# Decode attention with a gated feed-forward: how w_down, wo and the last V tiles are cut into DMAs

## The chip, the core and the metric

The kernel runs on one core of one Trainium2 chip. The metric is the time of one execution on the device in microseconds (us). The kernel before was timed in three runs: 2534.33 us median, from 2534.22 to 2534.78.

## The reference

One token attends over a cache of 65,536 positions with 32 heads of 128; a small feed-forward block works on the same token, and a scalar gate mixes the two. All inputs are bf16.

```python
# x: (1, 1, 512); k_cache, v_cache: (1, 32, 65536, 128); wq: (512, 4096); wo: (4096, 512)
q = (x @ wq).reshape(B, Sq, H, Dh).transpose(0, 2, 1, 3)
scores = jnp.einsum("bhqd,bhkd->bhqk", q, k_cache) * (Dh ** -0.5)
p = softmax(scores, axis=-1)
o = jnp.einsum("bhqk,bhkd->bhqd", p, v_cache)
a = o.transpose(0, 2, 1, 3).reshape(B, Sq, H * Dh) @ wo

# w_gate, w_up: (512, 1792); w_down: (1792, 512)
b = (silu(x @ w_gate) * (x @ w_up)) @ w_down

g = sigmoid((x * gate_w).sum(-1, keepdims=True))
out = g * a + (1 - g) * b
```

The two caches are 512 MiB each; everything else together is about 13 MiB.

## The kernel before, in words

**Tiles.** K and V of a head are each cut into four tiles of 16,384 positions, so there are N = 128 tiles of K and 128 of V. A tile is 128 partitions of 32 KB (NB = 128 positions of 128 values each), 4 MB in all. The tiles live in a ring of five slots of that size (`take` hands out the slot that came free first, `give` returns one). Weights that are needed for a while borrow a ring slot: wq in the beginning (`wq_t`), then w_gate and w_up together (`gu_t`), w_down (`wd_t`), and at the end the second half of wo (`wo_late`).

**Work on a tile.** For a K tile, VectorE multiplies it in place by q (L254) and halves the products by additions (L258); TensorE then adds the rest of each product in PSUM with the identity as weights (`scores`, L267), and VectorE folds four columns to one (L281). When a head's four tiles are scored, its softmax follows (L287 to L300). For a V tile, TensorE multiplies four columns of weights at a time (`values`, L322, 32 matmuls a tile). When a head's four V tiles are done, its 4x512 sums are copied (L335), turned into a column (`head_turn`, L351), scaled (L358) and multiplied by the head's rows of wo (`project`, L365) into two PSUM rows that gather all heads.

**The order.** The code is written in the order in which every engine works (`manual_schedule`). First four K tiles are scored, with the queries, the gate and the feed-forward block in between; then a loop over `steps` loads K tile n, the rows of wo that are due, and V tile v, and works on both. V runs some tiles behind K, so the last steps hold V alone.

**SP's queue.** Every large transfer is issued by SyncE (SP), in program order; SP waits at a DMA until its slot is free. The DMAs take eight completion semaphores in turn, the two small ones of ScalarE's queue at the start first, so an issue also waits until the DMA eight places ahead of it has landed. Up to the loop, SP's queue holds in this order: wq's first columns (L100), K tiles 0 to 2 (L110), the rest of wq (L382), w_gate (L387), K tile 3 (L110), w_up (L389), six DMAs of w_down (L402), K tile 4, two more DMAs of w_down, V tile 0; then K tile 5 and V tile 1, K tile 6 (into w_down's slot, so behind the matmuls of L233), the first wo rows (L163), V tile 2, and so on.

**w_down before.** Its 1792 rows lie on 64 partitions of 28 rows (28,672 contiguous bytes each). Eight DMAs carry it, each with eight partitions, one out of every four (first, first + 4, ... first + 28, for first = 0, 1, 2, 3, 32, 33, 34, 35). Since the hidden vector comes out on 128 partitions of 14 values (`hT`), two matmuls with every other column of the identity (L227) and a copy (L231) bring it to 64 partitions of 28, and 28 matmuls (L233) follow.

**wo before.** Heads 0 to 15 come four at a time (`WG = 4`), 512 KB in rows of 1 KB, one step or so ahead of use. Heads 16 to 31 (`LATE = 16`) come as 2 MB in four DMAs (L169) behind the last V tile, in cuts of 5, 5, 4 and 2 heads; their projections all run at the very end (L480).

**The last V tiles before.** V tiles 125 and 126 come in two halves, V tile 127 in pieces of 32, 32, 32, 16, 8 and 8 positions (`V_CUTS`). The last eight positions are not multiplied with the rest but turned at once into the head's column (L343).

The lines that the prediction's steps touch: `load` (L104 to L111), `load_wo` and `load_late` (L160 to L170), `feed_forward_out` (L223), `project` (L362), the start of the queue (L380 to L416), the loop (L432 to L481) and the output (L484 to L486).

Of the kernel before, what the change touches and what calls it, by code (L numbers as in the profile page):

```python
# [8 lines left out]
ACT = mybir.ActivationFunctionType  # L9
ALU = mybir.AluOpType  # L10
AXIS = mybir.AxisListType
P = 128
# [3 lines left out]
NB = 128  # L16
# [6 lines left out]
LAG = 8  # L23
SPREAD = 40

WG = 4
LATE = 16
LATE_CUTS = (0, 5, 10, 14, LATE)
TURNED = 8
V_CUTS = {3: (0, 64, NB), 2: (0, 64, NB), 1: (0, 32, 64, 96, 112, NB - TURNED, NB)}  # L30


@with_exitstack
def kernel(
# [14 lines left out]
    nc = tc.nc  # L49
    bf16 = mybir.dt.bfloat16  # L50
    f32 = mybir.dt.float32

    _, H, Sk, Dh = A_k_cache.shape
    D = A_x.shape[2]
    F = B_w_gate.shape[1]
    KT = D // P
    FT = F // P
    G = Sk // (NB * P)
    NBH = Sk // P
    N = H * G  # L60
# [4 lines left out]
    consts = ctx.enter_context(tc.tile_pool(name="consts", bufs=1))  # L65
# [7 lines left out]
    psum_m = ctx.enter_context(tc.tile_pool(name="psum_m", bufs=2, space=bass.MemoryType.PSUM))  # L73
# [7 lines left out]
    def take(name):  # L81
        slot = free.pop(0)
        held[name] = slot
        return ring.tile(
            [P, NB * Dh], bf16, name=name.split(".")[0], tag=f"slot{slot}"
        )

    def give(name):
        free.append(held.pop(name))
# [14 lines left out]
    def load(dst, cache, n, name, cuts=(0, NB), slot=None):  # L104
        h, g = divmod(n, G)
        t = take(f"{name}.{n}") if slot is None else slot
        view = t.rearrange("p (j d) -> p j d", d=Dh)
        src = cache[0, h, g * NB * P : (g + 1) * NB * P, :].rearrange("(p j) d -> p j d", j=NB)
        for a, b in zip(cuts[:-1], cuts[1:]):
            nc.sync.dma_start(out=view[:, a:b, :], in_=src[:, a:b, :])  # L110
        dst[n] = view  # L111

    def load_k(n):
        load(K_tiles, A_k_cache, n, "K_t")

    def load_v(n):
        load(V_tiles, A_v_cache, n, "V_t", V_CUTS.get(N - n, (0, NB)))

# [9 lines left out]
    ident_b = consts.tile([P, P], bf16, name="ident_b")  # L128
# [29 lines left out]
    wo_tiles = {}  # L158

    def load_wo(g):  # L160
        wo_tiles[g] = wo_pool.tile([P, WG, D], bf16, name="wo_sb", tag="wo_sb")
        rows = A_wo[g * WG * P : (g + 1) * WG * P, :]
        nc.sync.dma_start(out=wo_tiles[g], in_=rows.rearrange("(h p) n -> p h n", p=P))  # L163

    def load_late(cuts):
        late = take("wo_late.0")[:, : LATE * D].rearrange("p (h n) -> p h n", n=D)
        rows = A_wo[(H - LATE) * P :, :].rearrange("(h p) n -> p h n", p=P)
        for a, b in zip(cuts[:-1], cuts[1:]):
            nc.sync.dma_start(out=late[:, a:b, :], in_=rows[:, a:b, :])  # L169
        return late  # L170

    def feed_forward_in():
        gu_ps = psum_m.tile([P, 2 * FT], f32, name="gu_ps", tag="misc")
        for w in range(2):
            cols = wgu_sb[:, w].rearrange("p t (m c) -> p t c m", c=FT)
            for ft in range(FT):
                for t in range(KT):
                    nc.tensor.matmul(
                        gu_ps[:, w * FT + ft : w * FT + ft + 1],
                        lhsT=cols[:, t, ft, :],  # L180
                        rhs=xT[:, t : t + 1],
                        start=(t == 0),
                        stop=(t == KT - 1),
                    )
        gu_sb = consts.tile([P, 2 * FT], f32, name="gu_sb")
        nc.scalar.activation(out=gu_sb, in_=gu_ps, func=ACT.Copy)
        eg = consts.tile([P, FT], f32, name="eg")
        nc.scalar.activation(out=eg, in_=gu_sb[:, :FT], func=ACT.Exp, scale=-1.0)
        return gu_sb, eg
# [32 lines left out]

    def feed_forward_out(hT, rest):  # L223
        b_ps = psum_m.tile([1, D], f32, name="b_ps", tag="misc")
        h_ps = psum_m.tile([HP, GT], f32, name="h_ps", tag="misc")
        for r in range(2):
            nc.tensor.matmul(  # L227
                h_ps[:, r * FT : (r + 1) * FT], lhsT=ident_b[:, r::2], rhs=hT, start=True, stop=True
            )
        h2 = consts.tile([HP, GT], bf16, name="h2")  # L230
        nc.scalar.activation(out=h2, in_=h_ps, func=ACT.Copy)  # L231
        for t in range(GT):
            nc.tensor.matmul(  # L233
                b_ps, lhsT=h2[:, t : t + 1], rhs=wd_sb[:, t, :], start=(t == 0), stop=(t == GT - 1)
            )
        nc.scalar.activation(out=b_sb, in_=b_ps, func=ACT.Copy, scale=rest)
        for i, a in enumerate(a_ps):
            nc.tensor.matmul(  # L238
                a, lhsT=ones_f[0:1, 0:1], rhs=b_sb[:, i * HD : (i + 1) * HD], start=True, stop=False
            )  # L240
# [22 lines left out]
    def scores(n):  # L263
        S = F_tiles[n] = psum_s.tile([P, NB, QUAD], f32, name="S_ps")
        width = width_of(n)
        for c in range(0, width, QUAD):
            nc.tensor.matmul(  # L267
                S,
                lhsT=ident_b,
                rhs=K_tiles[n][:, :, c : c + QUAD],  # L270
                start=(c == 0),
                stop=(c == width - QUAD),
            )
        del K_tiles[n]
        give(f"K_t.{n}")
# [84 lines left out]
        )  # L360

    def project(h):  # L362
        rows = wo_tiles[h // WG][:, h % WG, :] if h < H - LATE else wo_late[:, h - (H - LATE), :]
        for i, a in enumerate(a_ps):
            nc.tensor.matmul(  # L365
                a,
                lhsT=oT[:, h : h + 1],
                rhs=rows[:, i * HD : (i + 1) * HD],
                start=False,
                stop=(h == H - 1),  # L370
            )


    def score_tile(n):
        for _ in products(n):
            pass
        if n:
            fold(n - 1)
# [11 lines left out]
    score_tile(1)  # L390
    xs = gate_sum()
    scores(1)
    wd_t = take("wd_t.0")
    HP = P // 2
    GT = F // HP
    wd_sb = wd_t[:HP, : GT * D].rearrange("p (t n) -> p t n", t=GT)
    wd_rows = B_w_down.rearrange("(p t) n -> p t n", t=GT)
    firsts = (0, 1, 2, 3, 32, 33, 34, 35)

    def load_wd(i):  # L400
        part = slice(firsts[i], firsts[i] + 29, 4)
        nc.sync.dma_start(out=wd_sb[part], in_=wd_rows[part])  # L402

    for i in range(6):
        load_wd(i)
    for g in range(1, H // QG):
        queries(g)
    give("wq_t.0")
    eg2 = gate_exp(xs)
    load_k(4)  # L410
    load_wd(6)
    load_wd(7)
    score_tile(2)
    rest = gate_value(eg2)
    scores(2)
# [7 lines left out]
    v = 0  # L423
# [5 lines left out]
        steps.append((None, v))  # L429
        v += 1  # L430

    done = tot_ps = wo_late = None  # L432
    for n, v in steps:
        if n is not None and n > G:
            load_k(n)
        if v is not None:
            if v % (WG * G) == 2 and v // (WG * G) < (H - LATE) // WG:
                load_wo(v // (WG * G))
            if v:
                load_v(v)  # L440
            if v == N - 1:
                wo_late = load_late(LATE_CUTS)
        vector = iter(()) if n is None else products(n)
        top_of = None
        if n is None:
            top_of = H - 1 if F_tiles else None
        elif n % G == 0:
            top_of = n // G - 1
            vector = (i for a in (0, NB // 2) for i in products(n, a, a + NB // 2))
        if top_of is not None:  # L450
            next(vector, None)
            fold(top_of * G + G - 1)
            mT_ps = row_max(top_of)
            next(vector, None)
            exponentials(top_of, mT_ps)
        if n == G:
            hT = feed_forward_mid(*ff)
        for _ in vector:
            pass
        if n is not None and n % G:  # L460
            fold(n - 1)
        if tot_ps is not None:
            weight(*tot_ps)
            tot_ps = None
        if n == G:
            feed_forward_out(hT, rest)
            give("wd_t.0")
        if done is not None:
            head_turn(done, head_copy(done))
        if v is not None:  # L470
            values(v)
        if top_of is not None:
            tot_ps = top_of, total(top_of)
        if n is not None:
            scores(n)
        if done is not None and done < H - LATE:
            project(done)
        done = v // G if v is not None and v % G == G - 1 else None
    head_turn(H - 1, head_copy(H - 1))
    for h in range(H - LATE, H):  # L480
        project(h)  # L481

    out_sb = consts.tile([1, D], bf16, name="out_sb")
    nc.vector.tensor_copy(out=out_sb[:, :HD], in_=a_ps[0])  # L484
# [32 lines left out]
```

## Time and profile before

| | |
|---|---|
| median of three runs | 2534.33 us |
| the profiled execution's own time | 2534.41 us |
| its span, first to last instruction | 2532.6 us |
| mean granted TensorE clock | 0.772 |
| VectorE busy | 2083.7 us (82%) |
| TensorE matmul busy | 1533.7 us (61%) |
| ScalarE busy | 77.7 us (3%) |
| DMA packets of SP's queue, share of 16 engines' span | 99.7% |
| read from HBM | 1087.64 MB |

The span is followed from the first to the last instruction; 1.8 us of the profiled execution's time lie around it. The profile gives busy times of the engines, a row of 40 slices with the DMA rate, the chain of work that ended last, and windows of any stretch with the mean busy share of the 16 DMA engines. Beside these views the trace has a record of every DMA packet: its start, its length, its bytes and its queue. All times in the text are from the span's start.

```
L322 PE MATMUL O_ps<-V_t,P_sb 128*4 128x512 bf16 x4094 | 1154.5, 452 | 663.5 <-DMA V_t<-in_A_v_cache_dram 663.5
L254 DVE TENSOR_TENSOR K_t<-K_t,q_bc 128x16384 bf16<-128x16384 bf16 (+1 forms) x159 | 1117.2, 7026 | 357.9 <-DMA K_t<-in_A_k_cache_dram 346.7
L233 PE MATMUL b_ps<-wd_t,h 64*1 64x512 bf16 x28 | 12.1, 625 | 0.3 <-ACT h L231 0.3
```

Each row is a group of instructions: line, engine, operation, tiles and count, then busy time and mean duration in ns of one, then the engine's idle time before them and what ended it. Both large groups waited for DMAs.

### The profile page before, as it was taken

Reading aid. Unit: us, or ns where it says so; the run is one execution under the profiler, and the core shown is the slowest. Engines: PE = TensorE matmul, PEld = TensorE weight load, DVE = VectorE, ACT = ScalarE, POOL = GpSimd, SP = SyncE. Lnnn points to the kernel's source line nnn. Section 1 sums busy time; section 2 is a strip of 40 time slices with the busy share of each in tenths; the row PEclk is TensorE's granted clock in tenths of the full one; section 3 lists DMA queues with packets and bytes.
Section 4 is the critical chain, followed back from the end, with each engine's and each line's share of the span. In section 5 each row is a group of like instructions: output and inputs, shape, how many; then the busy total and the mean of one; then the engine's idle time right before and its main releaser. Section 6 shows DMA issues by size and latency. Waiting matters only on the chain.

```text
span 2532.6 us, 13195 instructions
## 1 busy us (share of the span) xinstructions
PE 1533.7 (61%) x5786; PEld 581.6 (23%) x5786; DVE 2083.7 (82%) x744; ACT 77.7 (3%) x208; POOL 0.9 (0%) x7
## 2 busy tenths in 40 slices
PE   4656656665566555555665566556656665665569
PEld 1222222222222112222222122222222221222223
DVE  7788888888887999988888888888888888888860
ACT  1000000000000000000000000000000000000000
POOL 0000000000000000000000000000000000000000
PEclk9777777777777787787777777777777777777779
DMA  9999999999999999999999999999999999999998
GB/s 412 418 431 433 435 432 430 434 433 432 431 433 434 431 433 434 432 431 434 433 432 433 434 432 432 435 431 432 432 434 432 431 435 433 431 434 433 432 432 351
DMA packets 43915, 1088.49 MB, mean 430 GB/s; under 512 B 4753, under 2 KB 9362, under 8 KB 10258
## 3 DMA queue, kind: packets, MB, share of 16 engines
q1 hardware_dynamic: 43570, 1087.65, 99.7%
q8 instruction: 45, 0.74, 0.1%
q14 instruction: 12, 0.10, 0.0%
q10 hardware_dynamic: 288, 0.00, 0.0%
HBM read 1087.64 MB, written 0.00 MB: 429 GB/s over the span
## 4 chain that ended last, share of the span: by engine, by line
DMA 71%; PE 23%; DVE 4%; issue 1%; ACT 0%; SPq 0%; DVEq 0%
DMA V_t<-in_A_v_cache_dram 63%; PE O_ps L322 21%; DMA K_t<-in_A_k_cache_dram 8%; DVE K_t L254 3%; DVE K_t L258 1%; PE S_ps L267 1%; DMA wo_late<-in_A_wo_dram 0%; PE b_ps L233 0%; DVE S_sb L281 0%; DVE m L287 0%; PE oh_ps L351 0%; PE a_ps L238 0%; ACT P_sb L300 0%; PE a_ps L365 0%; PE mT_ps L291 0%
## 5 line engine op out<-in xcount | busy, mean ns | idle before, releaser
L322 PE MATMUL O_ps<-V_t,P_sb 128*4 128x512 bf16 x4094 | 1154.5, 452 | 663.5 <-DMA V_t<-in_A_v_cache_dram 663.5
L254 DVE TENSOR_TENSOR K_t<-K_t,q_bc 128x16384 bf16<-128x16384 bf16 (+1 forms) x159 | 1117.2, 7026 | 357.9 <-DMA K_t<-in_A_k_cache_dram 346.7
L258 DVE TENSOR_TENSOR K_t<-K_t 128x8192 bf16<-128x8192 bf16 (+1 forms) x314 | 859.7, 2738 | 8.6
L322 PEld LDWEIGHTS <-P_sb 128*4 128x4 bf16 x4094 | 393.0, 97 | 1405.1 <-issue 1064.1
L267 PE MATMUL S_ps<-K_t,ident_b 128*128 128x512 bf16 x1056 | 263.3, 393 | 100.6 <-DVE K_t L258 100.6
L267 PEld LDWEIGHTS <-ident_b 128*128 128x128 bf16 x1056 | 98.0, 101 | 248.0 <-issue 158.0
L291 PE MATMUL mT_ps<-diag,ones_f 128*128 128x128 f32 x64 | 24.5, 483 | 150.1 <-ACT diag L289 150.1
L351 PE MATMUL oh_ps<-ident_f,O_sb 4*128 4x1 f32 x256 | 55.5, 334 | 74.5 <-ACT O_sb L335 74.5
L281 DVE TENSOR_REDUCE S_sb<-S_ps 128x128 f32<-128x512 f32 x128 | 87.5, 683 | 4.9 <-PE S_ps L267 4.9
L289 ACT ACTIVATE diag<-ident_f,m 128x128 f32<-128x128 f32 x32 | 12.8, 401 | 2118.7 <-DVE m L287 2118.7
L351 PEld LDWEIGHTS oh_ps<-ident_f,O_sb 4*128 4x128 f32 x256 | 52.8, 301 | 84.1 <-ACT O_sb L335 82.9
L291 PEld LDWEIGHTS mT_ps<-diag,ones_f 128*128 128x128 f32 x64 | 15.2, 295 | 166.7 <-ACT diag L289 166.7
L484 DVE CAST out_sb<-a_ps 1x256 bf16<-1x256 f32 x1 | 0.4, 412 | 56.6 <-PE a_ps L365 56.6
L300 ACT ACTIVATE P_sb<-S_sb,bias 128x512 bf16<-128x512 f32 x32 | 23.1, 722 | 1.0
L287 DVE TENSOR_REDUCE m<-S_sb 128x1 f32<-128x512 f32 x32 | 22.0, 686 | 1.1
L335 ACT ACTIVATE O_sb<-O_ps 4x512 f32<-4x512 f32 x32 | 18.3, 572 | 129.2 <-PE O_ps L322 129.2
L313 DVE RECIPROCAL recip<-tot_ps 128x1 f32<-128x1 f32 x32 | 5.1, 158 | 13.0 <-PE tot_ps L308 13.0
L308 PEld LDWEIGHTS tot_ps<-rowsum,ones_f 128*128 128x128 f32 x64 | 9.5, 188 | 14.0 <-issue 14.0
L233 PE MATMUL b_ps<-wd_t,h 64*1 64x512 bf16 x28 | 12.1, 625 | 0.3 <-ACT h L231 0.3
L308 PE MATMUL tot_ps<-rowsum,ones_f 128*128 128x1 f32 x64 | 12.2, 260 | 0.0
L358 ACT ACTIVATE oT<-oh_ps,rg 128x1 bf16<-128x1 f32 x32 | 8.4, 263 | 65.0 <-PE oh_ps L351 65.0
L296 DVE TENSOR_REDUCE top<-mT_ps 128x1 f32<-128x128 f32 x32 | 9.1, 284 | 1.0 <-PE mT_ps L291 1.0
(47 smaller groups left out, 75.2 us busy)
## 6 DMA issues: line engine op xcount, KB each, us to landing
K_t<-in_A_k_cache_dram SPq DMA_DIRECT2D x128, 4096.0 KB, 35.3
V_t<-in_A_v_cache_dram SPq DMA_DIRECT2D x125, 4096.0 KB, 28.0
V_t<-in_A_v_cache_dram SPq DMA_DIRECT2D x4, 2048.0 KB, 31.1
wq_t<-in_A_wq_dram SPq DMA_DIRECT2D x1, 3584.0 KB
V_t<-in_A_v_cache_dram SPq DMA_DIRECT2D x3, 1024.0 KB
wo_sb<-in_A_wo_dram SPq DMA_DIRECT2D x4, 512.0 KB, 38.8
gu_t<-in_B_w_gate_dram SPq DMA_DIRECT2D x1, 1792.0 KB
gu_t<-in_B_w_up_dram SPq DMA_DIRECT2D x1, 1792.0 KB
```

Source lines behind the costliest of these rows:

```text
L254: yield nc.vector.tensor_tensor(out=K, in0=K, in1=q_rep, op=ALU.mult)
L258: yield nc.vector.tensor_tensor(out=K[:, :, 0:half], in0=K[:, :, 0:half], in1=K[:, :, half : 2 * half], op=ALU.add,)
L267: nc.tensor.matmul(S, lhsT=ident_b, rhs=K_tiles[n][:, :, c : c + QUAD], start=(c == 0), stop=(c == width - QUAD),)
L281: nc.vector.tensor_reduce(out=S_tiles[h][:, g * NB : (g + 1) * NB], in_=F_tiles.pop(n), axis=AXIS.X, op=ALU.add)
L287: nc.vector.tensor_reduce(out=m, in_=S_tiles[h], axis=AXIS.X, op=ALU.max)
L289: nc.scalar.activation(out=diag, in_=ident_f, func=ACT.Copy, scale=m)
L291: nc.tensor.matmul(mT_ps, lhsT=ones_f, rhs=diag, start=True, stop=True)
L300: nc.scalar.activation(out=P_tiles[h], in_=S_tiles[h], func=ACT.Exp, bias=bias, scale=scale, accum_out=rowsum[:, h : h + 1],)
L308: nc.tensor.matmul(tot_ps, lhsT=ones_f, rhs=rowsum[:, h : h + 1], start=True, stop=True)
L322: nc.tensor.matmul(O_tiles[h], lhsT=P_tiles[h][:, g * NB + j : g * NB + j + 4], rhs=V_tiles[n][:, j : j + 4, :], start=(g == 0 and j == 0) ...
L335: nc.scalar.activation(out=O_sb, in_=O_tiles.pop(h), func=ACT.Copy)
L351: nc.tensor.matmul(oh_ps, lhsT=O_sb[:, c * Dh : (c + 1) * Dh], rhs=ident_f[0:4, c : c + 1], start=(c == 0 and not turned), stop=(c == 3),)
```

## The change

Three things change together.

- **w_down** lies on 128 partitions of 14 rows. Its first row comes in nine DMAs: eight of eight partitions and 1 KB each (the same pattern of partitions as before, so 0 to 63), and one of partitions 64 to 127. One DMA on 128 partitions brings the other 13 rows (13,312 bytes a partition). All ten are issued behind K tile 4, not around it. K tile 4 gets the slot of K tile 1 and w_down that of wq, the other way round than before. The hidden vector needs no turning to 64 partitions, and 14 matmuls take the place of 28.
- **wo** comes two heads at a time (`WG = 2`), 256 KB in rows of 1 KB, for all 32 heads, in mid-run. Nothing comes behind the last V tile, and at the end only head 31 is left to project.
- **The last V tiles**: V tile 126 comes in four quarters, and the third quarter of V tile 127 in two pieces of 16 positions.

```diff
-WG = 4
-LATE = 16
-LATE_CUTS = (0, 5, 10, 14, LATE)
+WG = 2
 TURNED = 8
-V_CUTS = {3: (0, 64, NB), 2: (0, 64, NB), 1: (0, 32, 64, 96, 112, NB - TURNED, NB)}
+V_CUTS = {3: (0, 64, NB), 2: (0, 32, 64, 96, NB), 1: (0, 32, 64, 80, 96, 112, NB - TURNED, NB)}
...
-    def load_late(cuts):
-        late = take("wo_late.0")[:, : LATE * D].rearrange("p (h n) -> p h n", n=D)
-        rows = A_wo[(H - LATE) * P :, :].rearrange("(h p) n -> p h n", p=P)
-        for a, b in zip(cuts[:-1], cuts[1:]):
-            nc.sync.dma_start(out=late[:, a:b, :], in_=rows[:, a:b, :])
-        return late
...
-        h_ps = psum_m.tile([HP, GT], f32, name="h_ps", tag="misc")
-        for r in range(2):
-            nc.tensor.matmul(
-                h_ps[:, r * FT : (r + 1) * FT], lhsT=ident_b[:, r::2], rhs=hT, start=True, stop=True
-            )
-        h2 = consts.tile([HP, GT], bf16, name="h2")
-        nc.scalar.activation(out=h2, in_=h_ps, func=ACT.Copy)
-        for t in range(GT):
-            nc.tensor.matmul(
-                b_ps, lhsT=h2[:, t : t + 1], rhs=wd_sb[:, t, :], start=(t == 0), stop=(t == GT - 1)
+        for t in range(FT):
+            nc.tensor.matmul(
+                b_ps, lhsT=hT[:, t : t + 1], rhs=wd_sb[:, t, :], start=(t == 0), stop=(t == FT - 1)
             )
...
-        rows = wo_tiles[h // WG][:, h % WG, :] if h < H - LATE else wo_late[:, h - (H - LATE), :]
+        rows = wo_tiles[h // WG][:, h % WG, :]
...
-    wd_t = take("wd_t.0")
-    HP = P // 2
-    GT = F // HP
-    wd_sb = wd_t[:HP, : GT * D].rearrange("p (t n) -> p t n", t=GT)
-    wd_rows = B_w_down.rearrange("(p t) n -> p t n", t=GT)
-    firsts = (0, 1, 2, 3, 32, 33, 34, 35)
-
-    def load_wd(i):
-        part = slice(firsts[i], firsts[i] + 29, 4)
-        nc.sync.dma_start(out=wd_sb[part], in_=wd_rows[part])
-
-    for i in range(6):
-        load_wd(i)
     for g in range(1, H // QG):
         queries(g)
     give("wq_t.0")
     eg2 = gate_exp(xs)
     load_k(4)
-    load_wd(6)
-    load_wd(7)
+    wd_t = take("wd_t.0")
+    wd_sb = wd_t[:, : FT * D].rearrange("p (t n) -> p t n", t=FT)
+    wd_rows = B_w_down.rearrange("(p t) n -> p t n", t=FT)
+    for first in (0, 1, 2, 3, 32, 33, 34, 35):
+        part = slice(first, first + 29, 4)
+        nc.sync.dma_start(out=wd_sb[part, 0:1], in_=wd_rows[part, 0:1])
+    nc.sync.dma_start(out=wd_sb[P // 2 :, 0:1], in_=wd_rows[P // 2 :, 0:1])
+    nc.sync.dma_start(out=wd_sb[:, 1:], in_=wd_rows[:, 1:])
...
-            if v % (WG * G) == 2 and v // (WG * G) < (H - LATE) // WG:
+            if v % (WG * G) == 2:
                 load_wo(v // (WG * G))
             if v:
                 load_v(v)
-            if v == N - 1:
-                wo_late = load_late(LATE_CUTS)
...
-        if done is not None and done < H - LATE:
+        if done is not None:
             project(done)
...
     head_turn(H - 1, head_copy(H - 1))
-    for h in range(H - LATE, H):
-        project(h)
+    project(H - 1)
```

More of the change, by code (lines that the diff above doesn't have):

```diff
@@ L430 @@
         v += 1
-    done = tot_ps = wo_late = None
+    done = tot_ps = None
     for n, v in steps:
```

## The prediction

> **What bounds the kernel now.** I read the page's DMA rows first, then SP's waits, then windows of the end and of the start, then the chain of waits and the timeline of the last 30 us, and last the records of single DMA packets. The page:
>
> ```profile
> PE 1533.7 (61%) x5786; PEld 581.6 (23%) x5786; DVE 2083.7 (82%) x744; ACT 77.7 (3%) x208; POOL 0.9 (0%) x7
> ...
> q1 hardware_dynamic: 43570, 1087.65, 99.7%
> q8 instruction: 45, 0.74, 0.1%
> ```
>
> No compute engine is near full, and SP's queue q1 keeps the 16 DMA engines busy for 99.7% of the span. The time is the time in which the DMA engines move 1088 MB, and a change counts only by what it does to them or to what lies behind the last byte. The windows (their last two columns are the mean busy share of the 16 engines and GB/s) show where they are not full:
>
> ```profile
> 90.00:100.00 10.00, 10.00 (x24) 2.68 (x22) 6.45 (x4) 0.00 (x0) 0.00 (x0) 0.50 0.92 395
> 100.00:110.00 10.00, 9.23 (x32) 2.93 (x32) 9.97 (x2) 0.68 (x1) 0.00 (x0) 0.71 0.96 393
> ...
> 2515.00:2520.00 5.00, 5.00 (x25) 1.96 (x23) 0.00 (x0) 0.00 (x0) 0.00 (x0) 1.00 0.89 333
> 2520.00:2525.00 5.00, 4.54 (x27) 1.70 (x25) 0.00 (x0) 0.37 (x1) 0.00 (x0) 1.00 0.64 199
> ...
> 2527.00:2528.00 1.00, 1.00 (x12) 0.76 (x10) 0.00 (x0) 0.00 (x0) 0.00 (x0) 1.00 0.09 31
> 2528.00:2529.00 1.00, 0.94 (x10) 0.60 (x8) 0.00 (x0) 0.00 (x0) 0.00 (x0) 1.00 0.06 22
> ```
>
> At the end the engines do not stop together: a share of 0.06 is one engine of 16. That one engine, not their mean, sets the end.
>
> The packet records name it. On one engine a packet starts 3 or 4 ns before the one ahead of it ends, so packets can be strung into 16 chains in the order of SP's DMAs. A 32 KB packet takes 1.213 us, 28,672 B (w_down) 1.062, 14,336 B 0.535, 7,168 B 0.272, 1 KB 0.046, and a completion 0.009. The eight w_down DMAs put all their packets on the same eight engines: 8 x 1.065 = 8.5 us each. These engines start V tile 0 at 78.7 us, the other eight at 70.3. The others then run dry, since K tile 6 is issued only at 100.10 (SP waits 19.5 us for L233 to leave w_down's slot), so at V tile 3 they lead by 5.1 us (143.1 against 148.2). They lose that lead to the 45 packets of program code (q8): these go round eight engines, and each sets its engine back 1.41 us. Seven of the eight are not w_down's; one is. That one has both burdens, ends its last V piece at 2523.5 (the others at 2509.9 to 2518.4) and its last wo packet at 2528.94.
>
> Behind it stands the tail, here from the chain of waits and the timeline:
>
> ```profile
> 2516.42 12.18 DMA wo_late<-in_A_wo_dram
> ...
> 2528.65 1.48 PE a_ps L365 x12
> ...
> 2521.35 3.18 PE L322 MATMUL O_ps<-V_t,P_sb 128*4 128x512 bf16 x14 [0.28 <-DMA V_t<-in_A_v_cache_dram]
> ...
> 2524.63 0.59 ACT L335 ACTIVATE O_sb<-O_ps 4x512 f32<-4x512 f32 x1 [28.74 <-PE O_ps L322]
> ...
> 2525.27 1.05 PE L351 MATMUL oh_ps<-ident_f,O_sb 4*128 4x1 f32 x8 [0.46 <-ACT O_sb L335]
> ...
> 2526.35 0.26 ACT L358 ACTIVATE oT<-oh_ps,rg 128x1 bf16<-128x1 f32 x1 [1.14 <-PE oh_ps L351]
> ...
> 2530.15 0.37 ACT L485 ACTIVATE out_sb<-a_ps 1x256 bf16<-1x256 f32 x1 [3.54 <-PE a_ps L365]
> 2530.55 0.29 SPq L486 DMA_DIRECT2D out_dram<-out_sb  x1
> ```
>
> The copy, turn and scaling of the last head (L335, L351, L358) are over while wo still comes. From the last packet (2528.94) to the end (2532.6) there are 3.7 us.
>
> **The change part by part**, on the slowest engine.
>
> *w_down's bytes.* 70.3 to 78.7 us now: 8.4 us. After it, 128 partitions of 13,312 B are eight packets on every engine. Between the rows of 7,168 and 14,336 B that is 0.494 us each, 3.95 us. The first rows are 1 KB packets, 0.5 us an engine at most, and fall into the hole below.
>
> *The added wait.* The built program of the changed kernel shows what each DMA waits for. K tile 4 goes out when L267 is done with K tile 1 (46.4 instead of 57.01). The first five small ones need the queries (52.4); the sixth, K tile 3 (57.0); the seventh, w_up (62.3, since one engine ends w_up only at 61.84, behind code). The eighth waits for the DMA eight places ahead, and that is K tile 4 itself. Queued behind it on SP are the 64-row DMA, the large one, V tile 0, K tile 5, V tile 1. So when K tile 4 is through, the engines have seven 1 KB packets and then nothing. K tile 4 ends at 70.3, on the engine with code at 71.5; a landing is seen 0.34 later (K tile 3: last packet 56.61, chain 56.95): 71.9. Then two issues of 0.63 (median of L402) and 0.43 (L163's, the nearest for the 64 rows), and from issue to first packet 1.25 (K tile 6: 100.10 to 101.2 to 101.7 on idle engines): 74.15. Hole: 3.8 us. Engines that start together are slow at first: K tile 0 took 10.1 us, later tiles 9.68; I add 0.4: 4.2 us. Bounds: nothing, if the large DMA came in time; 5.4, by the slow restart at K tile 6 (K tile 6 took the dry engines 10.8 us, 1.1 over) and by issues of 0.79, the longest of L402. I take 4.2. w_down then costs 4.2 + 3.95 = 8.15 against 8.4: -0.2.
>
> *Fewer matmuls for w_down.* K tile 4 lands 6.4 us earlier (71.9; its product started at 78.44 after a landing at 78.25). From there to hT it takes 8.9 us (78.44 to 87.36), then 14 matmuls at 0.432 (L233: 12.1 us for 28): w_down's slot is free at about 87 instead of 100.1. V tile 1 ends on the engines at 78.5 + 29.1 = 107.6, so K tile 6 is issued 20 us ahead and the dip at 90 to 110 goes. That pays the dry engines 2.9 us, but they were not the last; the slow ones lost 0.3 there (19.7 us for two tiles, not 19.4): -0.3. If this cover were gone, up to 2.9 come back.
>
> *wo.* 2 MB leave the end and go before V's end: 128 packets of 42.3 ns, 5.4 us an engine in either place: 0. SP issues twelve more in mid-run (0.43 each) with 1174.6 us of waiting for L322 on its list, and the loads have no wait of their own. 32 matmuls of 0.27, 8.7 us, go into mid-run, where TensorE waits 663.5 us for V: 0.
>
> *Smaller pieces.* 16 KB packets take 0.611, 8 KB 0.309, 4 KB 0.159. Eight packets an engine of each piece: V tile 126 +0.06, V tile 127 +0.04; eleven more completions (eight wo, three V) of 6 ns: +0.2 in all.
>
> *Code.* Four or five engines get six code packets in either kernel: 0. The DMA end is thus -0.2 - 0.3 + 0.2 = -0.3: about 2528.6.
>
> *The tail.* Now a piece of V lands last, and the head's whole way is open behind it. Pieces of 16 land 3.8, 2.5 and 1.3 us ahead, that of 8 0.65; a matmul takes 0.22 (14 in 3.18), so TensorE keeps up and its last sum is there 0.25 us after the landing. From the rows, with their gaps: 0.34 landing + 0.25 + 0.69 copy + 1.10 turn + 0.29 scaling + 0.44 two matmuls + 0.40 copy + 0.03 + 2.08 from the output's issue to the end (2530.55 to 2532.63) = 5.6 against 3.7: +1.9.
>
> Sum: -0.3 + 1.9 = +1.6 on 2534.41, the profiled execution's time; on the median of 2534.33 it is **2535.9 us**.
>
> **The rivals.**
>
> *A. The slowest engine is not one of w_down's.* Then the change loads the engine that decides. For the other eight V tile 0 starts at 78.5 instead of 70.3, +8.2; they get back the 3.6 us lost up to V tile 3 (from V tile 0's start, seven tiles of 9.68 and a 512 KB wo DMA of 1.36 make 69.1, so 139.5 unhindered; 143.1 seen): +4.6, with pieces and tail +6.7: 2541.0, slower. It decides from where those engines end less than 2 us before the slowest. For it: seven of them carry code. Against it: they end at 2518.4 at the latest, 5 us ahead, if my chains are strung right; several engines ended packets within a few ns of each other, and there a string can cross.
>
> *B. No hole.* If the large DMA's packets are there when K tile 4 ends, 4.2 us go: 2531.7. For it: small packets need little time. Against it: the semaphore waits in the program.
>
> *C. TensorE lags in the last tiles.* At clock 0.50 a matmul takes 0.432 (L233), a V tile 13.8 us against 9.7 for its bytes; two such tiles put 8 us behind the last landing, where wo no longer covers them: 2544, slower. Against it: the granted clock is 1.00 in all windows from 2505 us on.
>
> *D. The small DMAs pay one by one.* If each of the three behind the wait takes a full round of issue, first packet and landing (0.63 + 1.25 + 0.34 = 2.2 us), the hole is 6.6 + 0.4, +2.8: 2538.7; with all nine in series it is 20 us and 2552. Against it: before, eight-partition DMAs of w_down follow each other on an engine within 6 ns. The Trainium skill (DMA: Bandwidth & Descriptors, section Rules for kernel authors) speaks for D: it says to merge small transfers, since those under 64 KB pay mostly overhead, and these have 8 KB. Where the queue is full the trace does not agree: those 6 ns.
>
> **How the numbers follow.** A difference under 0.2% (5.1 us, 2529.3 to 2539.4) counts as none here. Forecast 0.66 (none), B 0.09 (none), A 0.11 and C 0.05 (slower), D 0.05 (mostly none), other causes 0.04, of either sign. That makes none 0.78, slower 0.18, faster 0.04. The range goes from B's 2531.7, rounded to 2532, to just short of A, 2540.5; the forecast's own is 2532 to 2537.5 (hole from 0.5 to 5.4 us, tail 0.5 either way).
>
> **What would show it.** Right: windows between 70 and 75 us with a DMA share well under 0.9, SP waiting there at w_down's eighth small DMA for K tile 4; no dip at 90 to 110; K tile 6 issued before 90; the chain's last DMA a piece of V, at 2528 to 2529, then L335, L351, L358, L365 in a row and 5 to 6 us to the end. Wrong: no hole at 70 us (B), the last V piece after 2531 (A), L322 busy long after the last landing (C), a hole over 6 us (D).

## The result, and the profile after

| | us |
|---|---|
| before, median of 4 runs | 2534.27 (2534.22 to 2534.78) |
| after, median of 4 runs | 2547.70 (2547.34 to 2548.29) |
| ratio, 95% interval | 1.0054 (1.0040 to 1.0067) |
| span of the profiled execution | 2532.6 before, 2545.7 after |

The change costs 13.4 us. It was forecast at 2535.9, and the range ended at 2540.5. First the page of after, engines and queues:

```profile
PE 1526.3 (60%) x5769; PEld 578.8 (23%) x5770; DVE 2083.7 (82%) x744; ACT 77.5 (3%) x207; POOL 0.9 (0%) x7
...
q1 hardware_dynamic: 44354, 1087.66, 99.6%
q8 instruction: 45, 0.74, 0.1%
```

The bytes are the same and the DMA engines are still busy all the time: no engine took over the bound. SP's issues at the start (start, duration, engine, line, operation) and the windows around them show the hole behind K tile 4 where it was predicted:

```profile
46.07 0.33 SPq L108 DMA_DIRECT2D K_t<-in_A_k_cache_dram  x1
52.11 20.65 SPq L387 DMA_DIRECT2D wd_t<-in_B_w_down_dram  x8
72.80 0.52 SPq L388 DMA_DIRECT2D wd_t<-in_B_w_down_dram  x1
73.36 0.58 SPq L389 DMA_DIRECT2D wd_t<-in_B_w_down_dram  x1
74.06 0.36 SPq L108 DMA_DIRECT2D V_t<-in_A_v_cache_dram  x1
...
86.02 0.33 SPq L108 DMA_DIRECT2D K_t<-in_A_k_cache_dram  x1
```

```profile
65.00:70.00 5.00, 0.94 (x16) 0.88 (x16) 4.97 (x2) 0.41 (x2) 0.00 (x0) 0.50 0.97 419
70.00:75.00 5.00, 4.74 (x13) 1.68 (x13) 3.67 (x3) 0.00 (x0) 0.00 (x0) 0.55 0.28 59
75.00:80.00 5.00, 1.46 (x7) 0.53 (x5) 4.96 (x4) 0.40 (x1) 0.00 (x0) 1.00 0.98 399
...
90.00:100.00 10.00, 8.32 (x32) 2.93 (x31) 0.12 (x1) 0.00 (x0) 0.00 (x0) 0.75 1.01 436
100.00:110.00 10.00, 2.43 (x12) 1.00 (x11) 8.56 (x1) 0.00 (x0) 0.00 (x0) 0.76 1.02 439
```

```profile
SPq L387 <- DMA K_t<-in_A_k_cache_dram: 10.5, 2, 9.1
```

This row is from SP's waits between 40 and 110 us: at w_down's small DMAs (L387) it waited twice for a K tile, 10.5 us in all, the longer time 9.1. That longer wait is the eighth small DMA standing until K tile 4 had landed; its issue was over at 72.76 (52.11 + 20.65). The DMA share fell to 0.28 between 70 and 75, and the dip at 90 to 110 is gone. The timeline of the end of after (its code is shorter: L306 here is L322 of before, L460 is L486):

```profile
2539.11 1.46 PE L306 MATMUL O_ps<-V_t,P_sb 128*4 128x512 bf16 x6 [0.17 <-DMA V_t<-in_A_v_cache_dram]
...
2540.67 0.59 ACT L319 ACTIVATE O_sb<-O_ps 4x512 f32<-4x512 f32 x1 [28.47 <-PE O_ps L306]
2541.31 1.05 PE L335 MATMUL oh_ps<-ident_f,O_sb 4*128 4x1 f32 x8 [0.46 <-ACT O_sb L319]
2542.40 0.26 ACT L342 ACTIVATE oT<-oh_ps,rg 128x1 bf16<-128x1 f32 x1 [1.14 <-PE oh_ps L335]
2542.71 0.38 PE L349 MATMUL a_ps<-wo_sb,oT 128*1 128x256 bf16 x2 [0.35 <-ACT oT L342]
...
2543.53 0.28 SPq L460 DMA_DIRECT2D out_dram<-out_sb  x1
```

By the packet records the last V packet ends at 2539.94. From there to the end of the span it is 5.8 us (predicted 5.6). So start and end of the kernel went much as described, and the last byte still came 11.3 us late (2528.6 was forecast). That time is lost in the middle, where nothing seems to happen. Windows of mid-run, before and then after (last columns: TensorE clock, DMA share, GB/s):

```profile
200.00:800.00 600.00, 362.63 (x1326) 136.04 (x1325) 504.40 (x178) 17.26 (x48) 0.00 (x0) 0.76 1.00 433
800.00:1600.00 800.00, 469.44 (x1743) 174.82 (x1742) 701.67 (x245) 21.17 (x58) 0.00 (x0) 0.77 1.00 433
1600.00:2400.00 800.00, 483.50 (x1779) 183.09 (x1778) 672.96 (x240) 23.73 (x66) 0.00 (x0) 0.76 1.00 433
```

```profile
200.00:800.00 600.00, 358.19 (x1316) 135.07 (x1315) 502.17 (x176) 17.27 (x48) 0.00 (x0) 0.76 1.00 431
800.00:1600.00 800.00, 460.27 (x1724) 172.02 (x1722) 698.63 (x245) 21.18 (x58) 0.00 (x0) 0.76 1.00 431
1600.00:2400.00 800.00, 484.60 (x1782) 181.74 (x1780) 667.57 (x238) 21.99 (x61) 0.00 (x0) 0.76 1.00 431
```

The engines are busy for a share of 1.00 in both and move 433 GB/s before, 431 after: each packet takes longer. In the packet records from 200 to 2400 us, 99.8% of the 32 KB packets before last exactly 1213 ns; after, 5% do, and 93% last 1214 to 1224 (mean 1218.0). Over all 32 KB packets from 130 to 2480 us, the time above 1213 ns is 1.56 us an engine before and 9.68 after. Small packets of V tiles grow by some ns too (4 KB from 159 to 162.6, 8 KB from 309 to 314.1), so from 4 KB on it is a price per packet, not per byte; and a packet of program code (q8) grows from 930 to 1065 ns. Nothing in the diff names a cause.

### The profile page after: what moved, and what is told of

It reads as the page before. It is cut to its first block, busy times and chain, and to the rows that moved or that the text cites. A ratio compares the mean times of both kernels' runs of the same rounds, so it can differ in the third digit from the quotient of the medians.

```text
span 2545.7 us, 13166 instructions
## 1 busy us (share of the span) xinstructions
PE 1526.3 (60%) x5769; PEld 578.8 (23%) x5770; DVE 2083.7 (82%) x744; ACT 77.5 (3%) x207; POOL 0.9 (0%) x7
## 4 chain that ended last, share of the span: by engine, by line
DMA 72%; PE 22%; DVE 5%; issue 0%; ACT 0%; SPq 0%; DVEq 0%; ACTq 0%
DMA V_t<-in_A_v_cache_dram 66%; PE O_ps L306 21%; DMA K_t<-in_A_k_cache_dram 7%; DVE K_t L238 3%; DVE K_t L242 2%; PE S_ps L251 1%; DVE S_sb L265 0%; PE oh_ps L335 0%; DVE m L271 0%; ACT P_sb L284 0%; ACT O_sb L319 0%; PE mT_ps L275 0%; DVE top L280 0%; ACT diag L273 0%; PE a_ps L349 0%
## 5 line engine op out<-in xcount | busy, mean ns | idle before, releaser
L306 PE MATMUL O_ps<-V_t,P_sb 128*4 128x512 bf16 x4094 | 1155.2, 452 | 689.1 <-DMA V_t<-in_A_v_cache_dram 689.1
L306 PEld LDWEIGHTS <-P_sb 128*4 128x4 bf16 x4094 | 393.4, 97 | 1427.8 <-issue 1086.4
L349 PE MATMUL a_ps<-wo_sb,oT 128*1 128x256 bf16 x64 | 12.3, 275 | 0.4 <-ACT oT L342 0.4
```

The costliest lines, as they stand in the source:

```text
L306: nc.tensor.matmul(O_tiles[h], lhsT=P_tiles[h][:, g * NB + j : g * NB + j + 4], rhs=V_tiles[n][:, j : j + 4, :], start=(g == 0 and j == 0) ...
```

## The experiments

Unless a second one stands beside it, the mid-run line of a run is its window 200:800; the two later windows show the same rate in every run.

**Which part carries it.** e1 is the kernel before with w_down's part of the change alone, e2 the kernel before with the rest of it, wo and the V pieces, alone.

```diff
 # e1, on before: the hunks of the change in feed_forward_out and at load_wd, no others
-    for i in range(6):
-        load_wd(i)
...
+    for first in (0, 1, 2, 3, 32, 33, 34, 35):
+        part = slice(first, first + 29, 4)
+        nc.sync.dma_start(out=wd_sb[part, 0:1], in_=wd_rows[part, 0:1])
...
 # e2, on before: all other hunks
-WG = 4
-LATE = 16
+WG = 2
...
```

> The kernel before with w_down alone as in the changed kernel. Theory S (step): with w_down spread evenly all 16 DMA engines run in step, and in step a 32 KB packet takes about 1.218 us instead of 1.2138 in mid-run; then this edit carries nearly the whole loss but for the tail's 2 us: about 2545.5 us, mid-run rate 431 GB/s. Theory W (the sixteen small wo DMAs slow the packets): about 2534, rate 433. Theory H (only the dry stretch at 70 us costs): about 2535 to 2537, rate 433.

> The changed kernel with w_down as before, so wo and the last V tiles alone are changed. Theory S: the eight w_down engines stay apart from the others, mid-run rate 433 GB/s, only the tail's 1.9 us and 0.2 for smaller pieces come on: about 2536.4 us. Theory W: about 2545 us, rate 431. Theory H: 2536.4.

Mid-run of e1, then of e2:

```profile
200.00:800.00 600.00, 355.62 (x1317) 134.68 (x1316) 501.77 (x176) 17.27 (x48) 0.00 (x0) 0.76 1.00 431
200.00:800.00 600.00, 362.49 (x1326) 136.41 (x1326) 503.64 (x178) 17.27 (x48) 0.00 (x0) 0.76 1.00 433
```

e1: 2545.12 us (2544.87 to 2545.33), ratio to before 1.0044 (1.0029 to 1.0059), 431 GB/s. e2: 2535.46 (2534.53 to 2536.41), ratio 1.0005 (0.9996 to 1.0015), 433 GB/s. The slow packets come with w_down's part. wo and V cost 1.4 us by the medians, an amount that e2's interval doesn't tell from none. Theory S had foretold both runs rightly; W and H, which gave e1 433 GB/s, are out.

**w_down's queue order.** e3 is the kernel before with w_down in one DMA on 128 partitions at its old place; e4 adds six useless DMAs to the changed kernel, to set the two groups of eight engines apart.

```diff
 # e3, on before (and 14 matmuls as in after)
-    for i in range(6):
-        load_wd(i)
+    nc.sync.dma_start(out=wd_sb, in_=B_w_down.rearrange("(p t) n -> p t n", t=FT))
...
-    load_wd(6)
-    load_wd(7)
 # e4, on after, in the loop behind load_k(5)
+            if v == 1:
+                spare = wd_t[:, FT * D : FT * D + 8704]
+                rows = A_wq.rearrange("(p t) f -> p (t f)", t=KT)
+                for first in (0, 1, 2, 3, 32, 33):
+                    part = slice(first, first + 29, 4)
+                    nc.sync.dma_start(out=spare[part], in_=rows[part, :8704])
```

> The kernel before with w_down as one DMA on 128 partitions at its old place: no small DMAs, no wait for K tile 4, no dry stretch, old slots, 14 matmuls, wo and V as before. Theory S: the engines run in step, rate 431 GB/s; minus 4.2 us of w_down on the slowest engine, plus 8 to 9 of pace: about 2538 to 2540 us. Theory H, and any in which the small DMAs, the order or the slots do it: rate 433, about 2530 us, faster than before.

> The changed kernel with six further DMAs of eight partitions of 17,408 bytes each behind K tile 5, into a part of w_down's slot that nothing reads; they add 3.9 us of packets to eight engines and nothing to the other eight, and change no result. Theory S: the two groups are apart again, rate back to 433 GB/s and the time down by 4 to 8 us, to 2540 to 2544, though bytes are added. Theories W and H: rate 431, time the same or up to 4 us longer (2547.7 to 2552).

e3's mid-run:

```profile
200.00:800.00 600.00, 365.53 (x1325) 136.68 (x1325) 501.39 (x178) 17.27 (x48) 0.00 (x0) 0.76 1.00 431
```

e3: 2540.08 us (2539.90 to 2540.91), ratio 1.0025 (1.0016 to 1.0035), 431 GB/s: no hole, no small DMA, and still the slow packets. That is a third hit for theory S. e4: 2549.82 (2549.43 to 2551.09), 431 GB/s: 3.9 us of skew (one group of eight engines behind the other) cured nothing. Here theory S missed by 6 to 10 us. A theory with three hits was wrong all the same: its hits only said that the runs with w_down on 128 partitions are slow.

**Skew, count of DMAs, TensorE's program.**

```diff
 # e5, on before: the same 64 partitions in one DMA
-    for i in range(6):
-        load_wd(i)
+    nc.sync.dma_start(out=wd_sb, in_=wd_rows)
 # e6, on e3: eight useless DMAs in the places of before's eight
+    for i in range(5):
+        load_spare(i)
...
     load_k(4)
+    for i in range(5, 8):
+        load_spare(i)
 # e7, on e3: the matmuls twice
+        for _ in range(2):
             for t in range(FT):
 # e8, on before
-    firsts = (0, 1, 2, 3, 32, 33, 34, 35)
+    parts = [slice(a, a + 25, 4) for a in (0, 1, 2, 3, 32, 33, 34, 35)]
+    parts += [slice(28, 32), slice(60, 64)]
```

> Kernel before with w_down on its 64 partitions as before, but in one DMA in place of eight, at the place of the first six. What has to be told apart is why the mean 32 KB packet of the mid-run takes 1.218 us (431 GB/s) in the changed kernel and in the runs with w_down on 128 partitions, and 1.213 (433 GB/s) in the kernel before. Theory S (the two groups of eight engines must be far out of step from w_down on): if this DMA's 64 packets lie on the same eight engines, the skew is as before, 433 GB/s and 2534.3 us. Theory R (the count of DMAs and packets in the queue decides, not the skew): nine DMAs fewer change the count, 431 GB/s and about 2542. If the 64 packets are spread over all 16 engines, each bears 4.3 us, there is no skew, and S gives 431 GB/s and about 2538.

> e3_wd_one_dma (w_down in one DMA on 128 partitions) with eight useless DMAs of eight partitions of 17,408 B behind it, in the places that the kernel before has for its eight (five ahead of K tile 4, three behind it): 5.3 us more on one group of eight engines, from 62 us on, so before the packets had been slow for long. Theory S: the early skew is what kept the kernel before fast, 433 GB/s, and the slowest engine bears 4.3 + 5.3 = 9.6 us in place of 8.5: 2535.4 us. If skew is not it: 431 GB/s and about 2543.5.

> e3_wd_one_dma with its 14 matmuls of w_down done twice (same result), so that TensorE's program and the time at which w_down's slot comes free, and with it the issue of K tile 6, are nearly as in the kernel before. Theory T (the late issue of K tile 6, which lets the engines run nearly dry at 100 us, or the length of TensorE's program, keeps the packets fast): 433 GB/s, 2532 to 2534 us. Theories S and R: nothing changes, 431 GB/s, 2540.

> Kernel before with w_down in eight DMAs of seven partitions and two of four, in place of eight of eight: if the rows of a small DMA go to the lowest-numbered engines, the eighth engine of the group has no w_down at all. By the reading of the kernel before, that engine alone bore both w_down (8.5 us) and six code packets (8.5 us) and ended 5 us behind all others. Expected if that is right and the packets stay fast: 433 GB/s, the last V piece at about 2518.4, the last wo packet near 2524, 2529.3 us, 5 us less than before. If another engine of the group is the one with code: 2534 to 2536.5. If the packets turn slow: 2537 or more.

Windows of e5 (first two lines), and of e8:

```profile
60.00:70.00 10.00, 5.62 (x91) 5.48 (x90) 9.96 (x3) 0.41 (x2) 0.00 (x0) 0.70 1.05 241
...
200.00:800.00 600.00, 359.23 (x1322) 135.08 (x1320) 504.37 (x177) 17.27 (x48) 0.00 (x0) 0.76 1.00 433
```

```profile
80.00:90.00 10.00, 1.07 (x4) 0.68 (x4) 9.86 (x11) 1.61 (x5) 0.00 (x0) 0.50 0.71 113
...
200.00:800.00 600.00, 361.82 (x1337) 135.42 (x1334) 501.96 (x178) 15.51 (x43) 0.00 (x0) 0.76 1.00 433
```

e5: 2535.69 us (2535.01 to 2536.09), all 16 engines busy with w_down (share 1.05, so no skew), and 433. That refutes theory S from the other side, and R with it. e6: 2544.36 (2543.63 to 2545.07), 431: skew by 5.3 us from 62 us on changes nothing. e7: 2539.88 (2539.84 to 2540.32), 431: T is out. e8: 2541.50 (2540.45 to 2541.61), 433 in mid-run. Its loss is early: the share is 0.71 and the rate 113 GB/s at 80 to 90 us. The four packets of a DMA on four neighbouring partitions took up to 5.27 us each in place of 1.06, and SP's list between 60 and 110 us has 13.9 us of waiting for w_down's DMAs ahead of the next tiles (4.9 in before). As a better w_down it failed, so what it was to show of the engine with both burdens stayed open.

**What all slow runs share.** Sorted by rate, before, e2, e5 and e8 (433) have w_down on 64 partitions, and with it the tile `h2` (56 B a partition, 64 with padding). After, e1, e3, e4, e6 and e7 (431) need no turning and have no `h2`. `h2` is allocated in `consts`, ahead of the ring. With it the ring's first slot begins, in the built program, at byte 30,976 of a partition, 121 x 256; without it at 30,912, which is 192 past a multiple of 256. The slots are 32,768 B apart, so all five share that remainder. Unused columns behind `hT` move the ring, and all that is allocated behind it, without any other change:

```diff
-        hT = consts.tile([P, FT], bf16, name="hT")
+        hT = consts.tile([P, FT + 32], bf16, name="hT")[:, :FT]    # e9 (after), e10 (before), e11 (e3)
+        hT = consts.tile([P, FT + 96], bf16, name="hT")[:, :FT]    # e12 (after)
```

> The changed kernel with one change that no engine sees: hT gets 32 unused columns behind it, so that everything allocated behind it in SBUF, the five ring slots among it, begins 64 B later. The reason: all runs with 431 GB/s (after, e1, e3, e4, e6, e7) lack the tile h2 (56 B, padded to 64), their ring slots begin at byte 30,912 of a partition, which is 192 past a multiple of 256; all with 433 GB/s (before, e2, e5, e8) have it and begin at 30,976, a multiple of 256. Theory A (the address of the destination in SBUF sets the duration of a packet): 433 GB/s, 32 KB packets at 1.213 to 1.214 us, and by the excess of 9.7 us against 1.6 an engine, 8.1 us less: 2539.6 us. Rival (the number or the order of the DMAs): nothing changes, 431 GB/s, 2547.7.

> The kernel before with the same 32 unused columns: its ring slots begin at byte 31,040, 64 past a multiple of 256, and not one DMA, wait or instruction is another. Theory A: the kernel before turns slow, 431 GB/s, 32 KB packets near 1.218 us, and 7.6 to 8.1 us more than before: about 2542. Rival: 433 GB/s and 2534.2.

> e3_wd_one_dma (the kernel before with w_down in one DMA on 128 partitions, 2540.1 us) with the 32 unused columns, so with ring slots on a multiple of 256 again. Theory A: 433 GB/s and 7.6 us less, 2532.5 us: w_down's bytes on all engines are then worth what the prediction's sum gave for them without a hole, and it is the fastest version so far, by 1.7 us. Rival: 431 GB/s and 2540.1.

> The changed kernel with 96 unused columns behind hT: ring slots at byte 31,104, a multiple of 128 but not of 256. If the slots must begin on a multiple of 256 (as the Trainium skill has it for the transactions that a descriptor is cut into: DMA: Bandwidth & Descriptors, section How a descriptor splits into AXI transactions): 431 GB/s and 2547.7 us. If a multiple of 128 is enough: 433 GB/s and 2539.6.

| run | slots past a multiple of 256 | us, median (range) | 32 KB packet, mean ns, 200 to 2400 us |
|---|---|---|---|
| before, as timed beside e9 to e12 | 0 | 2533.99 (2532.41 to 2534.56) | 1213.8 |
| e10, before, shifted | 64 | 2543.69 (2542.73 to 2544.58) | 1217.7 |
| after | 192 | 2547.70 (2547.34 to 2548.29) | 1218.0 |
| e12, after, shifted | 128 | 2547.61 (2547.50 to 2548.19) | 1218.2 |
| e9, after, shifted | 0 | 2537.40 (2536.99 to 2537.58) | 1213.8 |
| e11, e3, shifted | 0 | 2529.87 (2529.55 to 2530.55) | 1213.8 |

The mid-run windows of e10, and then of e9:

```profile
200.00:800.00 600.00, 355.42 (x1313) 134.41 (x1313) 501.15 (x176) 17.27 (x48) 0.00 (x0) 0.76 1.00 431
800.00:1600.00 800.00, 467.55 (x1729) 174.23 (x1728) 702.17 (x246) 21.17 (x58) 0.00 (x0) 0.76 1.00 431
```

```profile
200.00:800.00 600.00, 358.89 (x1326) 135.46 (x1325) 504.31 (x178) 17.26 (x48) 0.00 (x0) 0.76 1.00 433
800.00:1600.00 800.00, 471.99 (x1735) 174.96 (x1734) 701.78 (x245) 21.17 (x58) 0.00 (x0) 0.76 1.00 433
```

e10 decides it: the kernel before, with the same DMAs, waits and instructions, loses 9.7 us when everything behind `hT` begins 64 B later (ratio 1.0039, 1.0024 to 1.0054); e9 wins 10.3 us by the same 64 B. Both effects are some 2 us larger than theory A expected (2539.6 for e9, about 2542 for e10); it had counted the 32 KB packets alone. A multiple of 128 is not enough (e12). The wo tiles and the small tiles behind the ring move with it; e13 below tells the slots from them. e11 is the fastest version: 0.9985 of before (0.9975 to 0.9995), 4.1 us less (2532.5 was expected), which is still within the 0.2% that the prediction counted as none.

**Slots apart, and the hole alone.** e13 leaves slots 0 and 1 of the kernel before aligned and moves the other three; e14 is e9 with w_down in one DMA.

```diff
 # e13, on before
+        extra = 32 if slot == 1 else 0
         return ring.tile(
-            [P, NB * Dh], bf16, name=name.split(".")[0], tag=f"slot{slot}"
-        )
+            [P, NB * Dh + extra], bf16, name=name.split(".")[0], tag=f"slot{slot}"
+        )[:, : NB * Dh]
 # e14, on e9
-    for first in (0, 1, 2, 3, 32, 33, 34, 35):
-        part = slice(first, first + 29, 4)
-        nc.sync.dma_start(out=wd_sb[part, 0:1], in_=wd_rows[part, 0:1])
-    nc.sync.dma_start(out=wd_sb[P // 2 :, 0:1], in_=wd_rows[P // 2 :, 0:1])
-    nc.sync.dma_start(out=wd_sb[:, 1:], in_=wd_rows[:, 1:])
+    nc.sync.dma_start(out=wd_sb, in_=wd_rows)
```

> The kernel before with 64 unused bytes behind ring slot 1: slots 0 and 1 stay on a multiple of 256, slots 2, 3 and 4 begin 64 B past one (and so do the wo tiles). If the extra time belongs to the slot that a tile is written to: 32 KB packets of tiles in slots 0 and 1 at 1.213 us, in the others near 1.218, 432 GB/s in mid-run, and three fifths of the 9.7 us that e10_before_shift64 lost: about 2540. If an engine that has met misaligned tiles stays slow for all of them: 1.218 in every slot, 431 GB/s, 2543.7.

> The changed kernel with aligned slots (e9_after_shift64, 2537.4 us) and w_down in one DMA on 128 partitions behind K tile 4, in place of the nine small ones and the large one: no DMA waits for K tile 4 any more. By the prediction's hole of 4.2 us, less 0.3 for the larger packets: 2533.5. By e11_one_shift64 (2529.9) and what the wo and V parts cost alone (e2_wo_v_only, 1.4 over before): 2531.3, a hole of 6 us with what follows it. If the small DMAs cost nothing: 2537.4.

e13: 2537.50 us (2536.66 to 2538.76), 432 GB/s. With the packets strung into chains (14 of the 16 could be followed to the end), a packet into an aligned slot takes 1213.9 ns in the mean, into another 1215.6, and it does so for K and V tiles alike. The first packet of an aligned tile still takes 1216.7, the other seven 1213.0 to 1213.8. So the time belongs to the slot, with some carry-over into the next tile. A misaligned tile between aligned ones loses less than among its like: 2.6 ns over 1213 here, 3.7 in e10 (in both without the few packets that take over 1300 ns, which before has too). So e13 lost 3.5 us and not the expected 6; the mean over all its packets is 1.5 ns above before's where e10's is 3.9 above, which is about the same share as 3.5 of 9.7 us.

e14: 2532.09 (2531.84 to 2532.60), between its first two forecasts. From 70 to 75 us its DMA share is 1.10, where e9 has 0.33: the hole is gone. Hole and small DMAs cost 2537.40 - 2532.09 = 5.3 us.

## Why the prediction was wrong

**The step that failed** is the constant under every transfer: "A 32 KB packet takes 1.213 us". It was read from the kernel before and carried over to the changed one unasked, into the DMA end ("about 2528.6") and into "Four or five engines get six code packets in either kernel: 0". In mid-run it held only in the kernels whose ring slots begin on a multiple of 256 B. The change took `h2` out, and the prediction counted the matmuls that go with it but not its 64 B of SBUF, behind which the ring lies. No rival named it; a price per packet on 31,000 packets was not in the sum at all. In its place the runs showed 1218.0 ns for such a packet (1213.8 in before), and by the medians this cost 2547.70 - 2537.40 = 10.3 us. The last V packet ends 9.9 us later than in e9 (2539.94 against 2530.06); of that, 8.2 us are the 32 KB packets (9.68 - 1.50 an engine), about 0.8 six code packets of 0.135 us more each, and most of the rest the smaller packets (up to about 0.25 us a size).

**The rest of the sum** is judged by e9, which is the change on aligned slots: 2537.4 for a forecast of 2535.9. That this is close is in part luck: by the medians w_down's part cost 1.9 us where the prediction has -0.5 for it (-0.2 and -0.3), and the other parts cost 0.7 less than forecast.

- *The hole*: right in place and cause, too small. With e14 the hole and the small DMAs measure 5.3 us, where 4.2 less 0.3 for the larger packets of one DMA, 3.9, was expected; the upper bound was 5.4. In the trace of after the first packet of the large DMA starts at 74.6, not 74.15, and its 13,312 B packets take 0.59 us in the mean in the restart, where 0.494 was interpolated: 8 x 0.1 = 0.8 more.
- *w_down's bytes and the dip*: 8.4 us to 4.3 with one DMA, and 0.3 for the dip, make -4.4. e11 against before: -4.1; e14 against e2: -3.4. About right. K tile 6 was issued at 86.02 (forecast about 87), and the dip went.
- *wo, pieces and tail*: +2.1 in sum, +1.4 by e2's median. From the last packet to the end 5.8 us in after and 5.6 in e9 (5.6 forecast).
- *Rivals*: B (no hole) is out, as the DMA share fell to 0.28. D (small DMAs pay one by one) is out: the DMAs behind the wait went out 0.56 and 0.70 us apart, not 2.2. C (TensorE lags) is out: L306 ended at 2540.57, 0.6 us behind the last packet. A (another engine is the slowest) gave 2541.0, and after showed its sign of a last V piece past 2531, but for another reason: with aligned slots the same queue ends at 2530.06. "Wrong: ... the last V piece after 2531 (A)" was too narrow a reading of that sign.
- *The lead of the slowest engine*, which is the argument against A, was misread. In the packet records of before two more engines end their last V pieces late, at 2519.9 and 2521.8, so the slowest is 1.7 us behind the next and not 5. The windows hint at it too: a share of 0.13 from 2526 to 2527 us is two engines of 16. By distance A's condition was met. What speaks against A is e11: it puts 4.3 us of w_down on the other eight engines, and even with A's 3.6 us back it would have gained nothing had one of those been the slowest. It gained 4.1. (e8's forecast of 5 us less rests on the same misreading.)

The 13.4 us are thus 10.3 for the address, 1.9 for w_down's new DMAs (e9 less e2: the hole's 5.3, less what the bytes gave back) and 1.4 for wo, V pieces and tail (13.6 in sum; the medians come from runs at different times, and the two small terms are near the noise).

## What to carry to other kernels

When an edit removes or adds any tile, see which tiles lie behind it in SBUF and whether those that DMAs fill still begin on the same boundary; here 56 bytes (64 with padding) cost 10.3 us, three times what the rest of the edit cost. A kernel at DMA share 1.00 can still lose time: compare GB/s and the durations of like packets in both traces before looking for a wait. And try the shift alone, both ways, before a theory of queues: it takes one line and leaves every instruction where it was.

## What the runs showed of the hardware

- A 32 KB packet into SBUF whose slot begins 64, 128 or 192 B past a multiple of 256 took 3.9, 4.4 or 4.2 ns more in the mean (e10, e12, after) than the 1213.8 of aligned slots in before. The shift also moves the addresses from which the engines read these tiles, and no run here separates the two. The Trainium skill (DMA: Bandwidth & Descriptors, section How a descriptor splits into AXI transactions) says that a descriptor is split into transactions of 256 B, that a transaction must start on a multiple of 256, and that a descriptor which does not begin on one costs extra beats for the bytes ahead of its start. It words this for reading, where here the shifted side is the one that the DMA writes. The boundary agrees with the runs (e12). The count of beats does not: 2, 4 and 6 more beats of 32 B would be 2.4, 4.7 and 7.1 ns (an estimate from 1024 beats in 1213 ns), where the measured price hardly depends on the offset.
- The price is not there from the start, so the address alone doesn't make it. In after, with the same slots, nearly all 32 KB packets took 1213 ns from 10 to 60 us; from 60 to 70 us nine in ten took longer; from 80 us on, behind the hole, nine in ten took 1213 again; and from about 115 us on nearly all stayed slow. In mid-run of after one packet in four is 7 to 9 ns over, and two in three are 0 to 2 over. What turns the packets slow stays open, as does why a slot's neighbours in time matter (e13).
- In e5, w_down's packets for 64 partitions took 2.25 us (median) where they took 1.06 in before, with all 16 engines on them at once. In e8 four packets for four neighbouring partitions took up to 5.27 us each. The Trainium skill (SBUF — State Buffer, section Door 1: The DMA port swizzle (why `[64,N]` ≈ `[32,N]`)) has 64 partitions reach only half of the ports, and four neighbours a single one; both rows agree with that. before's pattern of every fourth partition, eight packets at 1.06 us each, avoids it.
